# Gated linear attention and a soft mixture of experts: the turns go ahead of the scores in the middle units

## The chip, the cores and the metric

The kernel runs on one core of a Trainium2 chip. The metric is the device time of one execution in microseconds. The profile is one execution recorded by the hardware profiler; its times count from the start of its span.

## What is computed

Per batch (4) and head (8), over 768 positions of dimension 48, a gated linear attention; its output, as 3072 tokens of 384, goes through a soft mixture of 8 experts with 4 slots each.

```python
f = 1.0 / (1.0 + np.exp(-f_logit))
for t in range(S):
    state = f[:, :, t, :, None] * state + np.einsum('bhd,bhe->bhde', k[:, :, t], v[:, :, t])
    y[:, :, t] = np.einsum('bhd,bhde->bhe', q[:, :, t], state)
x = y.transpose(0, 2, 1, 3).reshape(B * S, H * D)
logits = x @ phi                                   # 3072 x 32
d = softmax(logits, axis=0); slot_input = d.T @ x  # 32 x 384
slot_out[e] = np.maximum(slot_input[e] @ w1[e], 0) @ w2[e]
out = softmax(logits, axis=1) @ slot_out
```

All data is fp32; w1 and w2 are 12.6 MB each.

## The kernel before

The positions are cut into chunks of 128; a unit is one chunk of 16 of the 32 head sequences, so there are 12 units (`NU`), and units u and u+2 share sequences. Two heads lie above each other on the 128 partitions, and 8 such pairs of 128 columns make the 1024 columns of a unit's f, k and q; half 0 is the first 512 columns, half 1 the rest.

The work on one unit, by the names in the code:

- The decay. `d_exp` and `d_ln` (ScalarE) make the log decay in the buffer of f; `d_scan` (VectorE) sums it up along the chunk; `d_g` makes its exponential g and `d_p` that of its negative, p (ScalarE). `d_k` multiplies k by g, `d_q` multiplies q by p (GpSimd; VectorE for unit 0). `d_pend` (ScalarE) keeps the last column of p for the state. In this kernel p has a region of its own and g is written over f.
- The scores. `scores(u, w)` are 8 matmuls over 48 rows for half w, into the PSUM tile PD (two banks). `s_mask` (VectorE) applies the causal mask on the way to SBUF. Both halves use PD, so the second scores wait for the first mask; only unit 0 puts its second half into the banks PA.
- The turns. `kt` turns k by 8 transposes into PC, `kt_copy` (ScalarE) takes it to SBUF for `kv`, which forms the chunk's addition to the state; `state_t` and `state_2` (VectorE) update the state. `x_tr` turns the outputs of the unit before into PA[0] and PA[1], and `x_copy` takes them out, the first half on ScalarE, the second on VectorE.
- The outputs. `inter` (queries by the old state) and `intra` (values by the masked scores) add up in PB, and `y_copy` (ScalarE) takes them to SBUF.
- Routing, once per two units. `c_lg` forms the logits in PA[0], `c_max` and `c_exp` a running softmax over the tokens, `c_tr` turns two 128x128 weight tiles in PB[0], `c_pin` sums the slots in PA[1], and `c_join` folds that into `pin`.

Every step has a due time, and `run_atoms` emits all steps in the order of their due times; `keep_order` fixes that order on each engine. So each engine works off its list strictly in order, and what stands at its head blocks what follows. The due times are written in the table `OFF`, in units whose period is T = 8.6; the frame of unit u begins at u*T with its first scores. Within frame u the decay of unit u+1 is finished (g, p, both products) and that of unit u+2 begun (exponential, logarithm, scan). Due times of units 0 to 4 are written out singly. In the old frame TensorE's order is: scores 0, turns of k, turns of x of the unit before, (odd frames: `c_tr`), scores 1, (even frames: `c_pin`, `c_lg`), `kv`, `intra` 0, `intra` 1; `inter` stands behind scores 1 in odd units and ahead of it in even ones.

SP issues nearly all transfers, in the same order of due times. f, k, q and v have 3, 3, 3 and 2 buffers; a load waits for the last reader of its buffer, and everything behind it on SP waits too. The w1 units (768 KB each) go into `wr` through the loop; w2 goes into the regions of f, p, k, q, v as these fall free, and six last ones into `wr` when `up` has read it.

After unit 11 the tail runs: `t_psi`, `up` (slots by w1), `turn`, then `down` in two column parts: part 0 (256 columns, PD) and part 1 (128 columns, PB[0]), 16 steps each. `slot_out` scales a part, `slot_out2` sums it over the experts and copies it to `s4`. `c_ct` turns the token softmax weights. `combine(h, y)` multiplies them by part h for a third y of the tokens, one bank for each of four row groups; ScalarE copies two banks, VectorE (`combine_2`) the other two, and `store` writes it out. Steps of the second `down` stand between the combines.

## Time and profile before

| | us |
|---|---|
| median of 3 runs | 155.72 (155.66 to 155.74) |
| the profiled execution | 155.44 |
| its span, first to last instruction | 153.7 |
| busy: TensorE matmul / weight load | 138.1 / 109.4 |
| busy: VectorE / ScalarE / GpSimd | 104.3 / 94.3 / 58.5 |
| moved by DMA | 53.97 MB |

The span is the time from the first to the last instruction on the core; 1.74 us of the profiled execution lie around it. In the rows, PE is TensorE's matmul and PEld its weight load, DVE is VectorE, ACT is ScalarE, POOL is GpSimd, and SPq is SP's DMA issue. An fp32 matmul leaves two records of each kind, a transpose one. "issue" behind a gap means that the engine waited for nothing that the profile shows. Most operands are called `arena`, which is one SBUF tile that holds all regions, so a step is told by its line: L185 `d_exp`, L188 `d_ln`, L193 `d_scan`, L196 `d_p`, L202 `d_g`, L206 `d_k`, L210 `d_q`, L219 `kt`, L222 `kt_copy`, L230 `scores`, L239 `s_mask`, L252 `kv`, L274 `inter`, L283 `intra`, L294 `y_copy`, L299 `x_tr`, L305 `x_copy`, L469 `down`, L482 `slot_out2`, L501 `combine`, L513 `store`.

### The profile page before, as it was taken

The numbers are of one execution on the slowest core, as the hardware profiler recorded it, in microseconds if no ns is written. First come the engines' busy times: TensorE is split into PE (matmuls) and PEld (weight loads), VectorE is DVE, ScalarE is ACT, GpSimd is POOL, SyncE is SP. The second block draws the span as 40 slices with busy tenths as digits, with TensorE's granted clock in tenths as the row PEclk, the third lists the DMA queues.
The fourth block names the chain that finished last, engine by engine and source line by source line (L and its number), as shares of the span: only waits on it lengthen the run. The fifth ranks groups of instructions, "written<-read, shape, count | busy, mean of one in ns | idle before, by whom it ended". The sixth has DMA issues, their size and how long they took to land.

```text
span 153.7 us, 5505 instructions
## 1 busy us (share of the span) xinstructions
PE 138.1 (90%) x2392; PEld 109.4 (71%) x2392; DVE 104.3 (68%) x153; ACT 94.3 (61%) x182; POOL 58.5 (38%) x51
## 2 busy tenths in 40 slices
PE   7987999999889999999999999999889999997500
PEld 7976888989769898889879897877433556675400
DVE  6899686999579887896969887759510563146500
ACT  4998899997789796969596976334402121035400
POOL 7008585788556483909293655600000000000000
PEclk9999999999999999999999999999999999999965
DMA  4899999999999999999999939999999993009990
GB/s 153 279 364 421 402 408 406 412 409 411 410 404 415 401 410 398 393 401 389 397 410 406 388 113 374 412 419 420 417 417 337 422 422 156 0 4 420 409 386 32
DMA packets 13424, 53.97 MB, mean 351 GB/s; under 512 B 1488, under 2 KB 1616, under 8 KB 13008
## 3 DMA queue, kind: packets, MB, share of 16 engines
q1 hardware_dynamic: 13248, 53.02, 87.2%
q10 hardware_dynamic: 144, 0.52, 0.9%
q8 instruction: 20, 0.33, 0.9%
q14 instruction: 12, 0.10, 0.2%
HBM read 48.82 MB, written 4.72 MB: 348 GB/s over the span
## 4 chain that ended last, share of the span: by engine, by line


## 5 line engine op out<-in xcount | busy, mean ns | idle before, releaser
L210 POOL TENSOR_TENSOR arena<-arena 128x512 f32<-128x512 f32 (+1 forms) x15 | 28.6, 1908 | 38.9 <-ACT arena L196 28.4
L239 DVE TENSOR_TENSOR arena<-pd,mask 128x1024 f32<-128x1024 f32 x23 | 27.8, 1210 | 10.2 <-PE pd L230 10.2
L193 DVE TENSOR_TENSOR_SCAN arena<-again,arena 128x512 f32<-128x512 f32 (+1 forms) x17 | 30.3, 1787 | 3.3 <-ACT arena L188 3.3
L230 PE MATMUL pd<-arena 48*128 48x128 f32 x368 | 27.0, 285 | 1.6 <-DVE arena L239 0.6
L206 POOL TENSOR_TENSOR arena<-arena 128x512 f32<-128x512 f32 (+1 forms) x15 | 27.6, 1852 | 0.4 <-POOL arena L206 0.4
L230 PEld LDWEIGHTS pd<-arena 48*128 48x128 f32 x368 | 22.3, 187 | 5.7 <-POOL arena L206 1.7
L283 PE MATMUL pb<-arena 128*48 128x128 f32 x384 | 23.5, 274 | 0.0
L283 PEld LDWEIGHTS pb<-arena 128*48 128x48 f32 x384 | 20.3, 123 | 1.1 <-issue 0.8
L196 ACT ACTIVATE arena<-arena 128x512 f32<-128x512 f32 (+1 forms) x17 | 13.6, 801 | 10.5 <-DVE arena L193 10.5
L294 ACT COPY arena<-pb 128x512 f32<-128x512 f32 x24 | 13.6, 584 | 6.6 <-PE pb L283 6.3
L185 ACT ACTIVATE arena<-arena 128x512 f32<-128x512 f32 (+1 forms) x16 | 13.5, 847 | 1.5 <-DMA arena<-in_f_dram 1.5
L202 ACT ACTIVATE arena<-arena 128x512 f32<-128x512 f32 (+1 forms) x17 | 13.8, 811 | 0.3
L188 ACT ACTIVATE arena<-arena 128x512 f32<-128x512 f32 (+1 forms) x16 | 13.5, 844 | 0.5
L299 PE MATMUL pa<-ident,arena 112*128 112x112 f32 x96 | 11.6, 262 | 0.3 <-ACT arena L294 0.3
L274 PE MATMUL pb<-arena 48*48 48x128 f32 x320 | 10.9, 274 | 0.0
L299 PEld LDWEIGHTS pa<-ident,arena 112*128 112x128 f32 x96 | 9.7, 141 | 1.1 <-ACT arena L294 0.7
L252 PE MATMUL pc<-arena 128*48 128x48 f32 x320 | 9.2, 210 | 0.9 <-ACT arena L222 0.9
L252 PEld LDWEIGHTS pc<-arena 128*48 128x48 f32 x320 | 8.1, 125 | 2.6 <-ACT arena L222 1.1
L219 PE MATMUL pc<-ident,arena 112*128 112x112 f32 x80 | 9.9, 266 | 0.0
L274 PEld LDWEIGHTS pb<-arena 48*48 48x48 f32 x320 | 8.4, 119 | 1.4 <-issue 0.2
L219 PEld LDWEIGHTS pc<-ident,arena 112*128 112x128 f32 x80 | 7.8, 141 | 1.9 <-issue 1.0
L165 PE MATMUL pd<-ones 128*128 128x128 f32 x50 | 7.3, 317 | 1.1 <-POOL ones L143 1.1
(140 smaller groups left out, 199.3 us busy)
## 6 DMA issues: line engine op xcount, KB each, us to landing
wr<-in_w_dram SPq DMA_DIRECT2D x22, 768.0 KB, 8.6
arena<-in_w_dram SPq DMA_DIRECT2D x10, 768.0 KB, 9.4
arena<-in_f_dram SPq DMA_DIRECT2D x10, 512.0 KB, 7.4
arena<-in_q_dram SPq DMA_DIRECT2D x10, 512.0 KB, 8.5
arena<-in_k_dram SPq DMA_DIRECT2D x10, 512.0 KB, 7.1
arena<-in_v_dram SPq DMA_DIRECT2D x12, 384.0 KB, 7.3
out_dram<-wr SPq DMA_DIRECT2D x3, 1024.0 KB, 4.8
arena<-in_f_dram SPq DMA_DIRECT2D x4, 256.0 KB, 4.1
```

The lines of the kernel that those rows point to most:

```text
L193: nc.vector.tensor_tensor_scan(t, cols(again, h), t, 0.0, op0=ALU.mult, op1=ALU.add)
L196: nc.scalar.activation(cols(R("p", u), h), cols(R("f", u), h), AF.Exp, scale=-1.0)
L202: nc.scalar.activation(cols(G(u), h), cols(R("f", u), h), AF.Exp)
L206: (eng or nc.gpsimd).tensor_tensor(t, t, cols(G(u), h), op=ALU.mult)
L210: (eng or nc.gpsimd).tensor_tensor(t, t, cols(R("p", u), h), op=ALU.mult)
L219: nc.tensor.transpose(PC[:, a // 4, 128 * (a % 4) : 128 * (a % 4) + W], kq[:W, a], ident[:W, :W])
L230: nc.tensor.matmul(t[:, 128 * p : 128 * p + 128], kq[rs, 4 * w + p], qq[rs, 4 * w + p], start=True, stop=True)
L239: nc.vector.tensor_tensor(dst, src, mask.unsqueeze(1).broadcast_to(list(dst.shape)), op=ALU.mult)
L252: nc.tensor.matmul(kvs[64 * r : 64 * r + D, a], kr[:, a, r], vb(u, a, r ^ a // 4), start=True, stop=True)
L274: nc.tensor.matmul(ys[a][o : o + D], heads(S0(u), D)[rs, a], qq[rs, a], start=p == 0, stop=False, skip_group_check=True,)
L283: nc.tensor.matmul(ys[4 * w + p][o : o + D], vb(u, 4 * w + p, r ^ w), sc[:, r, p], start=u < 2 and p == 0, stop=p == 3, skip_group_check=True,
L299: nc.tensor.transpose(PA[w][:, 128 * p : 128 * p + W], xTs[u][:W, w, p], ident[:W, :W])
```

## The change

1. Frames 4 to 9 (`BOTH`) take their due times from a second table, `OFF2`. TensorE's order there is: turns of k, turns of x, (`c_tr`), scores 0, scores 1, `inter`, (`c_lg`, `c_pin`), `kv`, `intra` 0, `intra` 1. The second scores of units 4 to 9 go into the banks PA[0] and PA[1], and their mask is two VectorE instructions of 512 columns instead of one of 1024.
2. p is written over f and g has the region of its own, everywhere; g and the product with k come before p and the product with q.
3. The second half of `x_copy` of units 3, 5 and 7 goes from VectorE to ScalarE (in the frames 4, 6 and 8).
4. Unit 5's logarithm stands behind the output copies of unit 3; its scan, both exponentials and products run by halves in frame 4. Unit 6's exponential and logarithm are placed by hand in that frame.
5. In the tail the turns of the second routing weights (`c_ct`) go from ahead of `down` step 8 to behind `slot_out(0)`; two steps of the second `down` stand ahead of the first combine instead of seven, then 5, 6 and 3 behind the combines instead of 3, 3 and 3; in `combine` the copy of the third bank is emitted after the first half of the matmuls.

```diff
+BOTH = range(4, 10)
+OFF2 = dict(
+    kt=0, xt=T + 0.82, tr=2 * T + 1.75, sc0=2.05, sc1=3.05, inter=4.15, lg=T + 5.2, pin=3 * T + 5.25, kv=5.4, intra0=5.7, intra1=6.6,
+    xe=T + 1.9, el=2 * T + 1.95, mask0=3.1, mask1=4.1, mx=T + 5.3, join=3 * T + 5.35, st=6.2, s2=6.3, scan=7.1 - 2 * T,
+    ktok=0.85, g=2.4 - T, p=3.5 - T, pend=4.6 - T, exp=4.7 - 2 * T, ln=5.8 - 2 * T, et=T + 6.0, y0=6.55, y1=7.55,
+    dk=3.0 - T, dq=4.4 - T,
+)
...
+    def d_g(u, h=None):
+        nc.scalar.activation(cols(R("g", u), h), cols(R("f", u), h), AF.Exp)
+
     def d_p(u, h=None):
-        nc.scalar.activation(cols(R("p", u), h), cols(R("f", u), h), AF.Exp, scale=-1.0)
...
+        nc.scalar.activation(cols(R("f", u), h), cols(R("f", u), h), AF.Exp, scale=-1.0)
...
-                rs, t = slice(64 * r, 64 * r + D), PD[:, r] if u or not w else PA[r]
+                rs, t = slice(64 * r, 64 * r + D), PA[r] if w and (not u or u in BOTH) else PD[:, r]
...
-        if u or not w:
+        if not w or u and u not in BOTH:
             parts = [(sc, PD.rearrange("p r (a t) -> p (r a) t", t=L))]
         else:
             parts = [(sc[:, 4 * r : 4 * r + 4], heads(PA[r], L)) for r in range(2)]
...
-            (nc.vector.tensor_copy if w and u < NU - 1 else nc.scalar.copy)(x, y)
+            (nc.vector.tensor_copy if w and u not in (3, 5, 7, NU - 1) else nc.scalar.copy)(x, y)
...
+            if n2 == 0:
+                combine_2(h, y, 2)
...
-        items += [(turn, 1, 0), (turn, 1, 1), (c_ct, 1)]
+        items += [(turn, 1, 0), (turn, 1, 1)]
         items += [(down, 0, *STEPS[x]) for x in range(8, 16)]
-        items += [(slot_out, 0)]
-        items += [(down, 1, *STEPS[x]) for x in range(3)]
-        items += [(slot_out2, 0)]
-        items += [(down, 1, *STEPS[x]) for x in range(3, 7)]
+        items += [(slot_out, 0), (c_ct, 1), (slot_out2, 0)]
+        items += [(down, 1, *STEPS[x]) for x in range(2)]
         for y in range(3):
...
-            items += [(down, 1, *STEPS[x]) for x in ((7, 8, 9), (10, 11, 12), (13, 14, 15))[y]]
+            items += [(down, 1, *STEPS[x]) for x in ((2, 3, 4, 5, 6), (7, 8, 9, 10, 11, 12), (13, 14, 15))[y]]
...
+        (2 * T + 2.955, d_exp, 5), (2 * T + 7.56, d_ln, 5), (3 * T + 2.0, d_scan, 5, 0), (3 * T + 2.1, d_g, 5, 0), (3 * T + 2.2, d_p, 5, 0),
+        (3 * T + 2.3, d_k, 5, 0), (3 * T + 2.4, d_q, 5, 0), (3 * T + 4.2, d_scan, 5, 1), (3 * T + 4.75, d_g, 5, 1), (3 * T + 4.76, d_p, 5, 1),
+        (3 * T + 4.77, d_k, 5, 1), (3 * T + 4.78, d_q, 5, 1), (3 * T + 4.8, d_pend, 5), (3 * T + 2.25, d_exp, 6), (3 * T + 4.7, d_ln, 6),
...
-    early = {(u, "inter"): u * T + 2.84 for u in (2, 4, 6, 8, 10, 11)}
+    early = {(u, "inter"): u * T + 2.84 for u in (2, 10, 11)}
```

(The times of the last list are counted from T, so 3 * T + 2.0 lies in frame 4.)

## Rows read from the trace of the kernel before

**Rows 1.** Stretches by frame; columns: engines' busy us (instructions), TensorE clock, DMA share, GB/s
```profile
38.91:49.26 10.35, 9.47 (x186) 7.81 (x184) 7.82 (x10) 8.60 (x18) 6.40 (x4) 1.00 1.03 410
...
49.26:56.98 7.72, 7.72 (x149) 6.94 (x147) 6.49 (x8) 6.39 (x11) 4.71 (x2) 1.00 1.03 409
...
56.98:66.12 9.14, 9.14 (x186) 7.81 (x184) 7.61 (x11) 7.23 (x14) 4.72 (x2) 1.00 1.01 396
...
82.98:90.70 7.72, 7.72 (x148) 6.93 (x146) 6.49 (x8) 6.34 (x10) 4.71 (x2) 1.00 0.83 323
```

**Rows 2.** Order of time, frame 5; columns: start, length, engine, line, operands, [idle before <-releaser]
```profile
49.26 0.97 PEld L230 LDWEIGHTS pd<-arena 48*128 48x128 f32 x16 [0.19 <-issue]
...
50.35 0.78 PEld L219 LDWEIGHTS pc<-ident,arena 112*128 112x128 f32 x8
```

**Rows 3.** Order of time: turns of k of unit 1, behind outputs
```profile
17.05 0.78 PEld L219 LDWEIGHTS pc<-ident,arena 112*128 112x128 f32 x8 [0.19 <-issue]
```

**Rows 4.** Order of time, frame 6: inter-chunk, then the second scores
```profile
59.75 0.84 PEld L274 LDWEIGHTS pb<-arena 48*48 48x48 f32 x32
...
60.77 0.97 PEld L230 LDWEIGHTS pd<-arena 48*128 48x128 f32 x16 [0.18 <-DVE arena L305]
```

**Rows 5.** Order of time, frame 4: logarithm, scan, second scores
```profile
39.13 1.06 ACT L188 ACTIVATE arena<-arena 128x1024 f32<-128x1024 f32 x1
...
40.29 2.45 DVE L193 TENSOR_TENSOR_SCAN arena<-again,arena 128x1024 f32<-128x1024 f32 x1 [1.54 <-ACT arena L188]
...
43.91 0.97 PEld L230 LDWEIGHTS pd<-arena 48*128 48x128 f32 x16 [0.73 <-DVE arena L239]
```

**Rows 6.** Order of time, ScalarE, frame 4: k copy, x copy, exponential
```profile
43.80 0.78 ACT L222 COPY arena<-pc 128x768 f32<-128x768 f32 x1
...
44.47 0.48 ACT L305 COPY arena<-pa 128x384 f32<-128x384 f32 x1
...
44.84 1.07 ACT L202 ACTIVATE arena<-arena 128x1024 f32<-128x1024 f32 x1
```

**Rows 7.** Order of time: scans on VectorE and products on GpSimd
```profile
34.86 1.72 DVE L193 TENSOR_TENSOR_SCAN arena<-again,arena 128x512 f32<-128x512 f32 x1
...
35.45 2.20 POOL L206 TENSOR_TENSOR arena<-arena 128x512 f32<-128x512 f32 x1
...
48.70 2.28 DVE L193 TENSOR_TENSOR_SCAN arena<-again,arena 128x1024 f32<-128x1024 f32 x1
...
54.55 2.37 POOL L206 TENSOR_TENSOR arena<-arena 128x1024 f32<-128x1024 f32 x1
...
56.49 2.58 DVE L193 TENSOR_TENSOR_SCAN arena<-again,arena 128x1024 f32<-128x1024 f32 x1
```

**Rows 8.** Order of time: second scores of unit 10
```profile
93.97 0.97 PEld L230 LDWEIGHTS pd<-arena 48*128 48x128 f32 x16 [0.42 <-DVE arena L239]
```

**Rows 9.** Groups by line and shape: count, busy us, mean ns, idle before
```profile
L305 DVE COPY arena<-pa 128x384 f32<-128x384 f32 x11 | 6.0, 548 | 0.5 <-PE pa L299 0.3
...
L239 DVE TENSOR_TENSOR arena<-pa,mask 128x512 f32<-128x512 f32 x2 | 1.3, 680 | 0.0
```

**Rows 10.** Order of time: last down steps, first combine, first store
```profile
134.00 0.81 PEld L469 LDWEIGHTS pb<-arena 128*32 128x32 f32 x32 [0.33 <-issue]
...
134.10 0.37 ACT L482 COPY s<-pd 128x256 f32<-128x256 f32 x1 [4.51 <-PE pd L481]
...
135.01 0.18 PEld L501 LDWEIGHTS pc<-s,ct 32*128 32x128 f32 x1 [0.20 <-issue]
...
136.89 0.18 PEld L501 LDWEIGHTS pd<-s,ct 32*128 32x128 f32 x1 [0.20 <-issue]
...
136.94 0.18 PEld L501 LDWEIGHTS pa<-s,ct 32*128 32x128 f32 x1
...
137.54 0.35 SPq L513 DMA_DIRECT2D out_dram<-wr  x1
```

**Rows 11.** Stretches: the output transfers at the end, columns as in the first group
```profile
138.50:149.50 11.00, 4.80 (x106) 3.43 (x94) 4.67 (x11) 3.59 (x6) 0.00 (x0) 0.91 1.00 404
```

More of the change, by code (lines that the diff above doesn't have):

```diff
@@ L47 @@
     lf=-1.7 - 3 * T, lk=4.0 - 3 * T, lq=6.4 - 3 * T, lv=-T,
-    exp=4.45 - 2 * T, ln=5.6 - 2 * T, scan=7.1 - 2 * T, p=1.0 - T, dq=2.05 - T, g=3.3 - T, dk=4.4 - T, pend=4.35 - T,
+    exp=4.45 - 2 * T, ln=5.6 - 2 * T, scan=7.1 - 2 * T, g=1.0 - T, dk=2.05 - T, p=3.3 - T, dq=4.4 - T, pend=4.35 - T,
     sc0=0, mask0=1.05, kt=1.1, ktok=1.95, sc1=2.85, mask1=3.95, inter=4.9, kv=5.4, intra0=5.7, st=6.2, s2=6.3, y0=6.55, intra1=6.6, y1=7.55,
@@ L97, in gla_soft_moe_kernel @@
     region("f", NF, 1024)
-    region("p", NP_, 1024)
+    region("g", NP_, 1024)
     region("kt", 1, 768)
@@ L490, in gla_soft_moe_kernel, with combine @@
     ]
-    def combine(h, y, last=(2, 3)):
+    def combine(h, y, last=True):
         hs_, wc = slice(CO[h], CO[h] + WC[h]), WC[h]
@@ L496, in combine @@
         banks = [two[:, 0], two[:, 1], b2, b3]
+        dst = stage[h][:, 2 * y : 2 * y + 2]
         for n2 in range(2):
@@ L501, in combine @@
                     nc.tensor.matmul(banks[n][:, wc * x : wc * x + wc], ct[ns, 2 * y + x], s4[ns, hs_], start=True, stop=True)
-        dst = stage[h][:, 2 * y : 2 * y + 2]
+            if n2 == 0:
+                combine_2(h, y, 2)
         nc.scalar.copy(dst[:, :, :2].rearrange("p v n d -> p n v d"), two[:, :, : 2 * wc].rearrange("p n (v d) -> p n v d", v=2))
-        for n in last:
-            combine_2(h, y, n)
+        if last:
+            combine_2(h, y, 3)
     def combine_2(h, y, n):
@@ L585, in gla_soft_moe_kernel @@
         (d_k, 0, 0, V), (d_q, 0, 0, V), (scores, 0, 0), (d_k, 0, 1, V), (d_q, 0, 1, V), (scores, 0, 1),
-        (load, "f", f, 3), (d_exp, 1, 0), (d_ln, 1, 0), (d_exp, 1, 1), (d_ln, 1, 1), (d_pend, 0), (kt, 0), (d_scan, 1, 0), (d_p, 1, 0), (d_scan, 1, 1), (kt_copy, 0),
-        (s_mask, 0, 0), (d_q, 1, 0), (d_g, 1, 0), (d_k, 1, 0), (d_p, 1, 1), (d_g, 1, 1), (d_k, 1, 1), (d_q, 1, 1), (s_mask, 0, 1), (kv, 0), (intra, 0, 0),
+        (d_exp, 1, 0), (d_ln, 1, 0), (d_pend, 0), (load, "f", f, 3), (d_exp, 1, 1), (d_ln, 1, 1), (kt, 0), (d_scan, 1, 0), (d_g, 1, 0), (d_scan, 1, 1), (kt_copy, 0),
+        (s_mask, 0, 0), (d_k, 1, 0), (d_p, 1, 0), (d_q, 1, 0), (d_g, 1, 1), (d_p, 1, 1), (d_k, 1, 1), (d_q, 1, 1), (s_mask, 0, 1), (kv, 0), (intra, 0, 0),
         (scores, 1, 0), (y_copy, 0, (0,)), (state_2, 0), (d_exp, 2, 0), (d_ln, 2, 0), (intra, 0, 1), (s_mask, 1, 0), (y_copy, 0, (1,)), (kt, 1),
-        (d_scan, 2, 0), (d_exp, 2, 1), (d_ln, 2, 1), (x_tr, 0), (d_pend, 1), (d_p, 2, 0), (d_q, 2, 0), (scores, 1, 1), (d_scan, 2, 1), (kt_copy, 1),
-        (d_g, 2, 0), (d_k, 2, 0), (s_mask, 1, 1), (d_p, 2, 1), (d_g, 2, 1), (d_k, 2, 1), (x_copy, 0), (intra, 1, 0), (kv, 1), (intra, 1, 1), (d_q, 2, 1),
+        (d_scan, 2, 0), (d_exp, 2, 1), (d_ln, 2, 1), (x_tr, 0), (d_pend, 1), (d_g, 2, 0), (d_k, 2, 0), (scores, 1, 1), (d_scan, 2, 1), (kt_copy, 1),
+        (d_p, 2, 0), (d_q, 2, 0), (s_mask, 1, 1), (d_g, 2, 1), (d_p, 2, 1), (d_k, 2, 1), (x_copy, 0), (intra, 1, 0), (kv, 1), (intra, 1, 1), (d_q, 2, 1),
         (state_2, 1), (d_pend, 2), (y_copy, 1), (d_exp, 3), (d_ln, 3),
@@ L615, in gla_soft_moe_kernel @@
         ):
-            if u < 2 or u == 2 and key in done or u in (3, 4) and key in ("exp", "ln", "scan", "p", "g", "dq", "dk") or u > NU - 3 and key in last_state:
+            if u < 2 or u == 2 and key in done or u in (3, 4, 5) and key in ("exp", "ln", "scan", "p", "g", "dq", "dk") or (u, key) in ((5, "pend"), (6, "exp"), (6, "ln")) or u > NU - 3 and key in last_state:
                 continue
-            at(early.get((u, key), z + o[key]), fn, u, *args)
+            frame = u - (2 if key in ("exp", "ln", "scan") else 1 if key in done else 0)
+            at(early.get((u, key), z + off(frame, key)), fn, u, *args)
         if 0 < u < NU - 1:
-            at(z + o["xt"], x_tr, u)
-            at(z + o["xe"], x_copy, u)
+            at(z + off(u + 1, "xt"), x_tr, u)
+            at(z + off(u + 1, "xe"), x_copy, u)
     for g in range(NV - 1):
@@ L625, in gla_soft_moe_kernel @@
         for key, fn in (("lg", c_lg), ("mx", c_max), ("et", c_exp), ("tr", c_tr), ("el", c_copy), ("pin", c_pin), ("join", c_join)):
-            at(z + o[key] - (T if g == NV - 2 and key in ("pin", "join") else 0), fn, g)
+            frame = 2 * g + (2 if key in ("lg", "mx", "et") else 3)
+            at(z + off(frame + (key in ("pin", "join")), key) - (T if g == NV - 2 and key in ("pin", "join") else 0), fn, g)
     at(-3, load_phi)
@@ L641, in gla_soft_moe_kernel @@
         [9 * T + 6.9, 10 * T + 6.9, 10 * T + 4.5, 10 * T + 4.6, 10 * T + 4.0, 11 * T + 4.0, 10 * T + 6.4, 11 * T + 6.4, 12 * T - 0.5],
-        span("f", 2) + span("p", 2) + span("k", 2) + span("q", 2) + span("v"),
+        span("f", 2) + span("g", 2) + span("k", 2) + span("q", 2) + span("v"),
     ))
```

22 lines of the change are left out of this document (10 added, 12 removed).

## The prediction

> **What bounds the kernel now.** I read the stretches by frame first: a frame runs from one unit's first scores to the next unit's. Frames 4, 5 and 6 last 10.35, 7.72 and 9.14 us, and the pair 7.72 and 9.14 repeats to frame 9; from 5 on TensorE is busy in all of it while VectorE, ScalarE and GpSimd are not (6.5, 6.4 and 4.7 of 7.72) [rows 1]. So TensorE's stream sets the loop: an odd frame has one piece more (two turns of the routing weights), an even one two (slot sums and logits). The transfers look full (share 1.01 to 1.03) but are not what waits: in frame 9 they run dry, at share 0.83 and 323 GB/s, and TensorE still takes its 7.72 us [rows 1].
>
> The time inside TensorE's stream that can be won is small. Weight loads are busy 6.94 of 7.72 us [rows 1]; the rest are gaps of 0.12 to 0.20 us where one piece ends and one of another operand shape begins. Scores to turns of k: 49.26 + 0.97 to 50.35, 0.12 us [rows 2]. Outputs to turns of k: 0.19 us at 17.05 [rows 3]. Inter-chunk to scores: 0.18 us [rows 4]. They stand there too where nothing was waited for ("issue"), so the change of shape makes them and not the wait.
>
> Frame 4 is another matter. ScalarE's logarithm of unit 5 ends at 40.19, the whole scan runs 40.29 to 42.74 behind it, the first mask comes after that on VectorE, and the second scores, which share the mask's PSUM tile, start at 43.91 after 0.73 us of idle loads [rows 5].
>
> From 138.5 on the output transfers are the bound (share 1.00, 404 GB/s for 11 us) [rows 11], so the end moves with the first store, at 137.54 [rows 10], as long as the next ones come in time.
>
> **Steady frames 5 to 9, part by part.** New TensorE order: turns of k, turns of the last unit's x, (routing turns), scores, scores, inter-chunk, (logits, slot sums), state, outputs. The gap between scores and the turns of k (0.12) goes. The gap before the turns does not: they now follow the outputs, and that costs the same 0.19 [rows 3] as outputs to scores did [rows 2]. The gap inter-chunk to scores (0.18) comes back as inter-chunk to logits. Scores to scores has one shape, bounded by 0 and 0.18; I take 0, since inside a run of one shape the 16 loads stand without a hole [rows 2]. So 0.12 us a frame: 7.60 and 9.02.
>
> Who could take this back? (a) The second scores now write the two banks that the x turns use, so they wait for both x copies. In even frames both are ScalarE's: the k copy can start at 1.02 into the frame (turns 0.98 long), the first x copy follows 0.67 later, the second 0.37 after it (44.47 behind 43.80 shows the first step, the next ScalarE instruction at 44.84 the second), end 0.48 on: 2.54 [rows 6]. TensorE gets there at 1.68 + 0.97 = 2.65, where 1.68 is both turns (59.75 - 56.98 - 1.09) [rows 1, 4]. Cover 0.1 us: thin, but enough. In odd frames VectorE copies one half behind its scan, ending near 2.0 + 0.55 = 2.55, against 2.9. (b) The second mask becomes two instructions of 0.68 [rows 9] for one of about 1.2 (42.74 to 43.91 in [rows 5]), so some 0.15 us more on VectorE, which idles 1.2 us a frame [rows 1]; taking a 0.55 us x copy [rows 9] off it in frames 4, 6 and 8 more than pays. Logits must wait for the first of them: 2.85 + 1.2 + 0.68 = 4.73, just when TensorE arrives. (c) GpSimd now does k before q. k is wanted at the frame's start, q 1.7 us later, so both products have cover; before, the second ended at 54.55 + 2.37 = 56.92, 0.06 us ahead of the scores it feeds at 56.98 [rows 1, 7]. (d) p now lives in the buffer of f, so the load of f three units on waits for the q product, up to 0.9 us into the next frame. SP holds the next v and w1 behind it. f is read in the second frame after, so this is free. Exchanging the exponentials of units 0 to 3 swaps equal instructions, and the scores still wait for the same second product: 0.
>
> **Frame 4.** Unit 5's exponential goes ahead into a ScalarE wait, its logarithm behind the y copies, its scan is cut in halves. TensorE: both turns to 38.91 + 1.68 = 40.59, first scores to 41.56. ScalarE: the last y copy of unit 3 follows the outputs that end about 38.95 (0.6 us, an estimate from 0.48 for the x copy's 384 columns [rows 6]) and ends about 39.6, logarithm 1.06 [rows 5] to 40.65, k copy, x copies at 41.3 and 41.65, to 42.15 [rows 6]. So the second scores start at about 42.2 instead of 43.91, still 0.6 late. Then scores and gap 1.09, inter-chunk 1.02 [rows 4], and what followed the second scores before, 49.26 - 43.91 - 1.09 = 4.26: 48.57. Frame 4 goes from 10.35 to 9.65: **-0.70**. Its bounds: 0 if the half scans and the final chain mask, join, state end late, -0.9 if the x copies were ready.
>
> **Frame 5** inherits a late VectorE. Unit 6's scan starts at about 48.2, at the same moment as GpSimd's last half product of unit 5. What two such cost each other: a half scan took 1.72 us over a half product of 2.20 [rows 7], where halves of 2.37 and 2.28 are 1.2 and 1.15; a whole scan with 0.43 us of overlap took 2.58 instead of 2.28 [rows 7]. So I add 0.65, nearer the half scan's, since the overlap is near 1.2 us: scan to 51.15, x copy to 51.7, while TensorE wants the bank at 48.57 + 2.9: 0.3 of stall. Frame 5: 7.72 - 0.12 + 0.3, **+0.17**.
> [...]
>
> **Frames 6 to 9**: 4 x 0.12 = **-0.48**. **Frame 10** returns to the old order with scores first, so unit 10 needs q at once. Scan to 2.0 into frame 9, exponential 1.06, two products of 2.37 [rows 5, 7]: about 7.95, where TensorE is ready at 7.60: **+0.35**. In exchange the second scores of unit 10, which stood 0.42 for the mask [rows 8] where a bare gap is 0.18, no longer do: **-0.24**. Loop: -0.70 + 0.17 - 0.48 + 0.35 - 0.24 = -0.90.
>
> **The end.** Seven steps of the second down projection stood before the first combine, now two; and the turns of the routing weights go from the wait for the j=1 mask to the wait for the scaled slots, so they fill another hole and cost nothing. The four steps behind the slot sum took 134.00 to 135.01, 0.20 each with a gap of 0.20 [rows 10]. With two the combine is bound by ScalarE's copy (134.10 + 0.37 = 134.47) [rows 10] and starts at 134.6 instead of 135.01: **-0.40**. Copying the third bank after half the matmuls gains nothing: the weights of the first bank (pd) and of the last (pa) go in within 0.05 us, at 136.89 and 136.94 [rows 10], so the four banks fill side by side. So the first store goes 0.4 earlier. The later combines move up to 0.55 back, because more steps now stand between them, but each 1 MB store hides 2.6 us of that. Bounds 0 to -0.6.
>
> **Sum.** -0.90 - 0.40 = -1.30. The profiled execution took 155.44 (span 153.7, 1.74 around it), the median is 155.72, so 154.14 and **154.4**.
>
> **Rivals.** (1) Slower: VectorE becomes the bound. Its busy time per pair of frames is 6.49 + 7.61 = 14.10 [rows 1]; with the masks' +0.30 and the x copy's -0.55 it is 13.85. If both whole scans of a pair ran wholly over GpSimd products, stretched like the half scan (1.72 for 1.2), they add some 1.6: 15.4; with 2.0 of its 2.76 idle us kept, since masks and state must wait for TensorE, a pair takes 17.4 against 16.86. Two and a half pairs: +1.4, frame 4 and the end give back 1.1, the wait at frame 10 is in it: **156.1**. It decides from the point where the scans end later than 2.6 into the frame. For it: the q product now reaches 0.3 to 0.9 us into the next frame. Against it: its overlap is 0.85 us and only every second frame. (2) No change: frame 4's stall only moves (late half scans, late join and state) and stores 2 and 3 starve the output queue. Gains 0.48 less 0.3: **155.5**. (3) More: score to score and outputs to turns both cost no gap, 0.19 in six frames: **153.3**.
>
> **How the numbers follow.** Forecast 0.55, (1) 0.18, (2) 0.15, (3) 0.12. Its own range is 153.7 to 155.2. With the rivals 153.2 to 156.2, which leaves out some 0.17. A measurement of this kernel tells 0.2% (0.3 us) from no change. Faster: forecast, (3) and a little of (2), 0.68; same 0.13; slower 0.19.
>
> **What would show it.** Right: odd frames near 7.6 and even ones near 9.0, each beginning with turns behind a 0.19 gap, no gap between the two scores; second scores of unit 4 near 42.2, waiting for ScalarE; scores of unit 10 waiting for GpSimd; first store 0.4 earlier relative to the last down step. Wrong: second scores waiting for x copies in most frames, scans of 2.8 us or more, a hole in the output transfers, or a frame 4 still over 10 us.

## The result and the profile after

The changed kernel takes **156.76 us** (median of 20 runs) against 155.95 for the kernel before, measured beside it: a ratio of 1.0056, 95% interval 1.0034 to 1.0078. It is slower by about 0.8 us where 1.3 us of gain was forecast. The profiled execution took 157.69 (span 155.9, 1.8 around it); it is one of the longer of its 20 runs, so it shows rather more loss than the median has.

In the rows of the changed kernel and of the runs made from it the lines are L201 `d_scan`, L215 `d_q`, L224 `kt`, L235 `scores`, L244 `s_mask`, L257 `kv`, L288 `intra`, L304 `x_tr`, L365 `c_pin`, L435 the copies behind `turn`, L468 `c_ct` and L474 `down`.

First the stretches by frame, as in [rows 1] (columns: engines' busy us, TensorE clock, DMA share, GB/s). Frame 4 is 39.61 to 50.71, the last row is frame 10.

```profile
39.61:50.71 11.10, 9.73 (x186) 8.17 (x184) 7.99 (x11) 9.06 (x18) 6.27 (x5) 1.00 1.02 410
50.71:58.23 7.52, 7.52 (x149) 6.86 (x147) 6.65 (x9) 6.67 (x10) 4.28 (x2) 1.00 1.01 395
58.23:67.26 9.03, 9.03 (x186) 7.75 (x185) 7.89 (x11) 7.96 (x15) 5.14 (x3) 1.00 0.99 380
67.26:75.39 8.13, 7.82 (x148) 6.91 (x146) 7.25 (x9) 6.68 (x10) 4.70 (x2) 1.00 0.99 377
75.39:84.42 9.03, 9.03 (x185) 7.75 (x184) 7.27 (x11) 7.86 (x15) 4.71 (x2) 1.00 1.02 400
84.42:92.42 8.00, 7.59 (x149) 6.86 (x147) 7.12 (x9) 7.03 (x11) 4.70 (x2) 1.00 0.77 311
92.42:100.50 8.08, 7.80 (x144) 6.33 (x144) 7.21 (x10) 3.61 (x9) 4.71 (x2) 1.00 0.87 322
```

The steady frames came as forecast: 7.52 for 7.72 and 9.03 for 9.14. Two frames did not: frame 4 grew from 10.35 to 11.10 instead of shrinking to 9.65, and frame 7 has 8.13. Frame by frame against before: +0.70 up to frame 4, then +0.75, -0.20, -0.11, +0.41, -0.11, +0.28, 0.00; from frame 11 to the last step of the first `down` part 0.00; from there to the end +0.44 (21.76 for 21.32). The +0.70 ahead of frame 4 is not the change: over all profiles here frame 4 begins between 38.91 and 39.74 with the old loop (six runs, mean 39.31) and between 38.86 and 39.80 with the new one (nine runs with the old warm-up, mean 39.31); in nine of these fifteen VectorE waits 0.2 to 1.0 us for the second half of unit 0's k.

The loss in frame 4 stands in TensorE's order of time, in the middle of the state matmuls `kv` (columns: start, length, engine, line, operands, [idle before <-releaser]):

```profile
45.78 0.83 PE L365 MATMUL pa<-arena,el 128*32 128x384 f32 x8
46.54 0.74 PE L257 MATMUL pc<-arena 128*48 128x48 f32 x23
48.61 0.42 PE L257 MATMUL pc<-arena 128*48 128x48 f32 x9 [1.33 <-issue]
```

TensorE stops after 23 of the step's 32 matmul records and goes on 1.54 us later (start to start), in a run of equal matmuls whose operands are all there. "issue" means that the profile shows nothing that was waited for. Frame 7 has a smaller one inside `intra`:

```profile
73.91 0.35 PEld L288 LDWEIGHTS pb<-arena 128*48 128x48 f32 x5
74.82 0.39 PEld L288 LDWEIGHTS pb<-arena 128*48 128x48 f32 x7 [0.56 <-issue]
```

Counted from the start of TensorE's records (matmuls, weight loads and its few waits, 4817 in all), both holes begin at a record that is 193 over a multiple of 256 (1473 and 2497), and so does the hole of 0.40 that the kernel before has inside its 16 scores at 40.47 (record 1217). The DMA queues have a row for code: 20 transfers, 0.33 MB, so 16 KB each; 20 blocks of 256 would hold the 4817 records. From 13 to 111 us exactly one of these transfers begins between each such block's end and the next.

```profile
q8 instruction: 20, 0.33, 0.9%
```

So I formed the **theory** that TensorE runs out of code: a block of 256 instructions is fetched by DMA, and where it comes late the engine stands at the block's end. In the trace the block that TensorE goes on with at 48.61 began to be fetched at 46.06, which is 4.96 us after the last block's end at 41.11; the transfer takes about 1.1 and another 1.5 pass until the engine goes on. Without holes a block lasts 5.8 to 7.3 us in the loop, 6.0 in frame 4, so by my estimate (6.0 less 1.1 and 1.5) a delay above about 3.5 is felt there. The **rivals**: the hole belongs to that place in the work; or the loss is the tail's.

### The profile page after: what moved, and what is told of

Its sections match the earlier page's. It is cut to its first block, busy times and chain, and to the rows that moved or that the text cites. A ratio compares the mean times of both kernels' runs of the same rounds, so it can differ in the third digit from the quotient of the medians.

```text
span 155.9 us, 5541 instructions
## 1 busy us (share of the span) xinstructions
PE 138.2 (89%) x2392; PEld 109.5 (70%) x2392; DVE 106.0 (68%) x157; ACT 98.0 (63%) x187; POOL 58.4 (37%) x53
## 3 DMA queue, kind: packets, MB, share of 16 engines
q1 hardware_dynamic: 13248, 53.02, 86.5%
## 4 chain that ended last, share of the span: by engine, by line
## 5 line engine op out<-in xcount | busy, mean ns | idle before, releaser
L201 DVE TENSOR_TENSOR_SCAN arena<-again,arena 128x512 f32<-128x512 f32 (+1 forms) x18 | 32.7, 1820 | 3.9 <-ACT arena L196 3.9
L215 POOL TENSOR_TENSOR arena<-arena 128x512 f32<-128x512 f32 (+1 forms) x16 | 28.9, 1804 | 0.0
L244 DVE TENSOR_TENSOR arena<-pd,mask 128x1024 f32<-128x1024 f32 x17 | 20.6, 1214 | 8.0 <-PE pd L235 8.0
L288 PE MATMUL pb<-arena 128*48 128x128 f32 x384 | 23.9, 274 | 0.3 <-issue 0.3
L288 PEld LDWEIGHTS pb<-arena 128*48 128x48 f32 x384 | 20.4, 123 | 1.6 <-issue 1.4
L235 PE MATMUL pd<-arena 48*128 48x128 f32 x272 | 19.8, 285 | 1.3 <-POOL arena L215 0.4
L235 PEld LDWEIGHTS pd<-arena 48*128 48x128 f32 x272 | 16.5, 187 | 4.5 <-POOL arena L215 1.8
L257 PEld LDWEIGHTS pc<-arena 128*48 128x48 f32 x320 | 8.2, 125 | 5.4 <-issue 4.3
L304 PE MATMUL pa<-ident,arena 112*128 112x112 f32 x96 | 11.7, 262 | 0.3 <-ACT arena L299 0.3
L257 PE MATMUL pc<-arena 128*48 128x48 f32 x320 | 9.4, 210 | 2.2 <-issue 1.3
L304 PEld LDWEIGHTS pa<-ident,arena 112*128 112x128 f32 x96 | 9.7, 141 | 1.1 <-ACT arena L299 0.7
L224 PE MATMUL pc<-ident,arena 112*128 112x112 f32 x80 | 9.9, 266 | 0.0
L227 ACT COPY arena<-pc 128x768 f32<-128x768 f32 x10 | 7.9, 792 | 1.9 <-PE pc L224 1.9
L244 DVE TENSOR_TENSOR arena<-pa,mask 128x512 f32<-128x512 f32 x14 | 9.0, 681 | 0.1
```

What stands on the lines that cost most here:

```text
L201: nc.vector.tensor_tensor_scan(t, cols(again, h), t, 0.0, op0=ALU.mult, op1=ALU.add)
L215: (eng or nc.gpsimd).tensor_tensor(t, t, cols(R("f", u), h), op=ALU.mult)
L235: nc.tensor.matmul(t[:, 128 * p : 128 * p + 128], kq[rs, 4 * w + p], qq[rs, 4 * w + p], start=True, stop=True)
L244: nc.vector.tensor_tensor(dst, src, mask.unsqueeze(1).broadcast_to(list(dst.shape)), op=ALU.mult)
L257: nc.tensor.matmul(kvs[64 * r : 64 * r + D, a], kr[:, a, r], vb(u, a, r ^ a // 4), start=True, stop=True)
L288: nc.tensor.matmul(ys[4 * w + p][o : o + D], vb(u, 4 * w + p, r ^ w), sc[:, r, p], start=u < 2 and p == 0, stop=p == 3, skip_group_check=True,
```

## The experiments

**Which half loses.** Two runs take the change apart: the new loop with the old end, and the old loop with the new end. (Edit: `tail` and `combine` of the one kernel put into the other.)

> The changed loop with the old end (old order of the down steps, weight turns and bank copies). The profile of the changed kernel had its first store 0.44 us earlier against the last step of the first down part, as predicted, but its last store 0.64 later and the end of the span 0.48 later (21.82 against 21.34). Theory (the new end costs about 0.4, because the last store sets the end): 156.3 against the changed kernel's 156.76. Rival (the new end gains the predicted 0.4 and the loop loses all): 157.2. Third (the end is worth nothing either way, stragglers of the last transfers): 156.8. The span from the last step of the first down part to the end tells the same in the profile: 21.3 (theory) or 21.8.

> The kernel before with the new end alone. Theory (new end costs 0.4): 156.4 against 155.95. Rival (gains the predicted 0.4): 155.55. Third: 155.95.

Measured: the new loop with the old end 1.0049 (1.0019 to 1.0079), the old loop with the new end 0.9978 (0.9956 to 1.0000). The loop is what loses; the end gains 0 to 0.7. That the end costs 0.4 fell; what it does is settled further down. The new loop has its hole again, at the same place in the state matmuls: 1.54 us, with the code fetched 5.07 after the block's end.

**Is the hole code?** One run leaves out four loads, so that less stands in the queues around frame 4; two others shift the block ends by 64 records.

```diff
     def load_w1(i):
         e, hf = W1[i]
         w1u[e, hf] = wr[:, i].rearrange("p (c x) -> p c x", c=3)
+        if i in (2, 3, 4, 5):
+            w1u[e, hf] = wr[:, 0].rearrange("p (c x) -> p c x", c=3)
+            return
```

> The changed kernel without the loads of four of the sixteen w1 units (the third to the sixth, 768 KB each, whose matmuls read the first unit instead), which leaves out 7.9 us of transfers in frames 3 to 5. Theory (code for TensorE comes late because its transfer stands behind data in busy queues): the code blocks start within 2 us of the last block's end in frames 3 to 5, there is no hole in unit 4's state matmuls, and frame 4 is at most 9.7 us instead of 11.10. Rival (code comes late for a reason of its own, or the hole isn't code): hole and frame stay, 11.1. The whole time falls by an amount that tells nothing, since transfers are left out.

Measured: the hole is gone. The stretches of frames 4 and 5, the step where the hole was, and the queues from the block's end at 40.76 (columns: transfers, which the profile's page calls packets, MB, share):

```profile
39.27:48.80 9.53, 9.49 (x186) 8.05 (x184) 7.58 (x11) 8.36 (x17) 5.04 (x5) 1.00 0.85 287
48.80:56.73 7.93, 7.78 (x148) 6.93 (x146) 6.97 (x9) 7.20 (x12) 7.78 (x3) 1.00 0.45 164
```

```profile
46.20 0.93 PE L257 MATMUL pc<-arena 128*48 128x48 f32 x32
```

```profile
q1 hardware_dynamic: 14, 0.04, 72.6%
q8 instruction: 1, 0.02, 41.4%
```

The code block was fetched 0.10 us after the last one ended, behind 14 data transfers, fewer than one for each of the 16 DMA engines; in the changed kernel 4.96 us, behind 517 (32 for each). Frames 4 to 10 sum to 59.12 against 59.87 before. So without late code the new loop is worth **0.75 us**; in the changed kernel they sum to 60.89. (The paced run further down keeps all transfers and has the same 59.12.)

The two shifts:

```diff
-        warm(25, PD[:, 1, :128])
+        warm(41, PD[:, 1, :64])
```

> The changed kernel with 41 warm-up matmuls of 64 columns ahead of the first scores instead of 25 of 128, so that every later TensorE instruction stands 64 records further on in the instruction stream (4 records each) and the work is the same. Theory (the holes of 1.46 us in the state matmuls of unit 4 and 0.56 in the outputs of unit 7 are TensorE running out of code: each hole stands where a fetched block of 256 instructions ends): those two places run through without a hole, and any hole of this kind stands 64 records earlier in the work (with a block's end at about 46.9 instead of 48.6 in frame 4, that is in the slot sums or before them). Rival (the holes belong to the work there, a wait that the profile doesn't show): they stay at the same matmuls. Time: theory, 156 to 157, by where the ends now fall; rival 156.8.

```diff
+    def pad(n):
+        for _ in range(n):
+            nc.tensor.matmul(PC[:, 1, 496:512], ones, ones[:, :16], start=True, stop=True)
...
-        (d_k, 0, 0, V), (d_q, 0, 0, V), (scores, 0, 0), (d_k, 0, 1, V), (d_q, 0, 1, V), (scores, 0, 1),
+        (d_k, 0, 0, V), (d_q, 0, 0, V), (scores, 0, 0), (pad, 8), (d_k, 0, 1, V), (d_q, 0, 1, V), (scores, 0, 1),
...                                         # and (pad, 8) behind (kt, 0)
```

> The changed kernel with 16 matmuls of 16 columns (64 records) added in two holes of TensorE ahead of 14 us, so that the ends of the code blocks stand 64 records earlier in the work, with the clock as it was. Theory (blocks of 256): no hole in the middle of unit 4's state matmuls nor in the outputs of unit 7; a hole, if the backlog still makes one, stands 64 records earlier, in unit 4's slot sums at about 46.5, or at the ends of the other blocks. Rival (the hole belongs to that place in the work): unit 4's state matmuls stop after 23 or 24 of 32 as before. Time by the theory 155.5 to 157, by the rival 156.8.

Measured: 169.11 and 163.84 us, so both times were missed by far, because TensorE was slow until 24 and 28 us (last section). In both, `kv` of unit 4 and `intra` of unit 7 run through, and no block end in frames 4 to 10 has a hole above 0.10. That speaks against a hole that belongs to its place. At the start of frame 4 as much had been moved as in the changed kernel (14.32 and 14.36 MB, 14.32 there), but the code came 3.31 and 3.19 us after the block's end instead of 4.96, so no hole shows at the shifted place either, and these two alone would not decide.

**With all transfers kept.** The w1 loads are spread otherwise, in the new loop and, as a control, in the old.

```diff
     for i in range(16):
-        at((1.6 + 0.62 * i) * T - 0.9, load_w1, i)
+        at((1.6 + 0.62 * (i + 2 * (3 <= i < 12))) * T - 0.9 if i not in (12, 13) else 9 * T + 6.8, load_w1, i)
```

> The changed kernel with the same transfers, but the w1 units from the fourth on are issued two places (10.7 us) later and the thirteenth and fourteenth go into the hole that the transfers have in frame 9 (10 GB/s from 91.5 to 94). Theory (the loop's loss is TensorE waiting for blocks of its code, which stand behind the backlog of data): without the loads of the four w1 units the same loop took 9.53, 7.93, 9.03, 7.52, 9.03, 8.00 and 8.08 us for frames 4 to 10, 59.12 against 59.87 before, so with a shorter backlog in frames 3 to 5 frame 4 is at most 9.7, the hole in unit 4's state matmuls goes, and the median is 155.95 - 0.75 - 0.1 (the end): 155.1. Rival (the holes only move to another frame as the loads come later): 156.7. Second rival (the loss in the median sits elsewhere, the hole is an accident of the profiled execution): 156.7 with all frames short.

> The kernel before with the same later w1 loads. Theory (in the kernel before the one late block of code, at 40.47, lies under the wait for the first mask, so there is nothing to win): 155.95, within 0.3. Rival (the later loads are worth something of themselves, so that a gain of the run before this is not the changed loop's): 155.2 or less.

Measured: 0.9995 (0.9970 to 1.0020) in the new loop, where the changed kernel has 1.0056, and 1.0005 (0.9979 to 1.0032) in the old. So the spread takes 0.6% off the new loop and nothing off the old: the hole was the loss. Frame 4 of the paced run, with the code now 3.61 after the block's end:

```profile
38.88:48.42 9.54, 9.50 (x186) 8.06 (x185) 7.59 (x11) 8.36 (x17) 5.09 (x5) 1.00 0.98 361
```

But 155.1 was missed by 1 us. The 0.76 that frames 4 to 10 give are there at the first `down` step (123.33 for 124.09), and 0.23 of them are left at the last step of its first part (132.15 for 132.38): TensorE, now early, stands for the last w2 units.

```profile
130.61 1.43 PEld L474 LDWEIGHTS pd<-wr,arena 128*32 128x32 f32 x26 [0.40 <-DMA wr<-in_w_dram]
```

The kernel before has no such wait. The transfers run full from 54 to 128 us here; the new pacing has a hole of its own at 50 to 54 (16 GB/s from 50 to 52). Two variants of the paced run: frame 9 in the old order (`BOTH = range(4, 9)`), and the old end.

> The later w1 loads of the first of these runs, and frame 9 in the old order (frames 4 to 8 alone begin with the turns). Theory (frame 9 costs 0.28 because unit 10, which begins with scores, finds its q product 0.41 late): frame 9 back to 7.72 and no wait for GpSimd ahead of unit 10's scores, 0.28 below the first run: 154.8. Rival (frame 9 in the old order gives back its turn gap of 0.12 and the stretched scan of unit 11 comes earlier anyway): equal to the first run within 0.1.

> The paced run of the changed loop (w1 two places later) with the old end. Theory (in the new end the turns of the weights cost 0.44 because they lost their cover, and with the old end they stand in the wait for the mask and for the last w2 units): 0.4 below the paced run with the new end (156.07), 155.65, and 21.3 instead of 21.76 from the last step of the first part. Rival (the end is the same either way, its transfers set it): 156.05.

Measured: 0.9991 (0.9965 to 1.0017) and 1.0007 (0.9982 to 1.0033), both equal to the paced run, so both theories missed their times. In the first, frame 9 is 7.71 instead of 7.99 and nothing stands before unit 10's scores, as expected; holes of 0.17 and 0.15 for code and the wait for w2 take it back. In the second the code block of frame 4 came 4.05 late and made a hole of 0.44, so it does not tell the ends apart.

**The end.** Old place for the weight turns, five steps instead of seven ahead of the first combine, in the old loop and in the new:

```diff
-        items += [(down, 1, *STEPS[x]) for x in range(3, 7)]
+        items += [(down, 1, *STEPS[x]) for x in range(3, 5)]
...
-            items += [(down, 1, *STEPS[x]) for x in ((7, 8, 9), (10, 11, 12), (13, 14, 15))[y]]
+            items += [(down, 1, *STEPS[x]) for x in ((5, 6, 7, 8, 9), (10, 11, 12), (13, 14, 15))[y]]
```

> The kernel before; of the second down part five steps instead of seven stand ahead of the first combine, the weight turns stay in their old place ahead of the last steps of the first part, and the two steps go between the first and the second combine. The first combine and the first store come 0.4 earlier (2.2 instead of 2.63 after the last step of the first part), the later combines and the last store stay (9.67; last store 12.74). Theory (the end follows the last store: in all profiles so far it comes 8.4 to 8.8 us after that store is issued): end 21.3 after the last step of the first part as before, time 156.0. Rival (the prediction's: the transfers are full, so the end moves with the first store): 20.9, time 155.6.

> The changed kernel with the end in which the weight turns stay in their old place and five steps stand ahead of the first combine. Theory (the new end gave back its 0.4 because the weight turns lost the wait that covered them; with it the output stream from first to last packet takes 13.66 us instead of 13.28): first combine still 2.2 after the last step of the first part, stream 13.28, last output packet 0.4 earlier than in the changed kernel, 156.3 against 156.76. Rival (the closing code after the last packet takes that up): 156.7.

Measured: 0.9993 (0.9963 to 1.0023) in the old loop, 1.0023 (0.9994 to 1.0053) in the new, which lies 0.3% under the changed kernel, with intervals that overlap. The traces say more. In five runs with the old end the output stream takes 13.27 to 13.30 us from its first to its last packet and ends 19.27 to 19.30 after the last step of the first part; in five with the new end (all but the shift runs and the one without four loads) 13.65 to 13.68 and 19.19 to 19.23; with this one 13.28 and 18.85 (old loop), 13.12 and 18.68 (new loop). So for the stream the prediction's rule (the first store moves it) held, the theory that the last store sets it fell, and the new end's stream has a hole. In the time it is not shown: the stream's 0.44 would be 0.9972 in the old loop, and the interval holds that as well as no change. First the old loop's stretch of full output with this end, then that of the changed kernel and the hole in it:

```profile
138.80:150.10 11.30, 5.39 (x118) 3.95 (x114) 5.10 (x11) 3.95 (x6) 0.00 (x0) 0.94 1.01 409
```

```profile
139.70:151.20 11.50, 5.96 (x142) 4.59 (x138) 5.10 (x11) 3.95 (x6) 0.00 (x0) 1.00 0.98 394
143.90:145.10 1.20, 0.84 (x24) 0.69 (x26) 0.21 (x1) 0.27 (x1) 0.00 (x0) 1.00 0.79 328
```

From the last packet to the end another 2.0 to 2.7 us pass, in which blocks of code are fetched again; they vary by more than what is to be told apart here, which is why single spans do not settle the end.

**All three causes together.** The changed loop without frame 9, this end, and w1 loads that leave no hole in the transfers; and, as a control, the same loads and end with the old loop.

```diff
-        at((1.6 + 0.62 * i) * T - 0.9, load_w1, i)
+        at(4 * T + 6.5 if i in (4, 5) else 9 * T + 6.8 if i > 12 else (1.6 + 0.62 * (i + (2 if i == 3 else i > 5))) * T - 0.9, load_w1, i)
```

> The changed loop with frame 9 in the old order, the end of the run before this, and w1 loads spread anew: the fourth a frame later, the fifth and sixth at the end of frame 4 where the paced runs had a hole in the transfers (16 GB/s from 50 to 52), the last three into the hole of frame 9. Theory (three things took the loop's 0.75 in turn: late code, then the last w2 units, which TensorE reached 0.35 ahead of their landing, then the turns of the weights out of their cover, 0.44): no hole for code, no wait for w2, end 21.3 after the first part's last step: 156.0 - 0.75 - 0.28 = 155.0, ratio 0.993 to 0.995. Rival (the transfers from 2 to 129 us are a bound of their own, so that TensorE's gains before them are lost in the wait for w2 whatever the order): 155.7 or more, with a wait for w2 of 0.3 or more.

> The fastest run's spread of the w1 loads and its end, with the loop of the kernel before. Theory (the changed loop is worth 0.75 to 1.0 once code and w2 come in time): 155.8 to 156.0, against 155.02 with the changed loop. Rival (the gain of that run is the spread of the loads and the end, the loop's order is worth nothing in the time): 155.0 to 155.3.

Measured: **155.02 us, 0.9924 (0.9898 to 0.9950)** with the changed loop, the fastest here, and 0.9979 (0.9952 to 1.0005) with the old one. So the loop, without frame 9, is worth about 0.55% (0.85 us; 0.2 to 0.9% by the two intervals together) once its code and w2 come in time. Its frames 4 and 5, and the sum of frames 4 to 10:

```profile
39.02:48.75 9.73, 9.69 (x186) 8.17 (x185) 7.78 (x11) 8.56 (x18) 5.27 (x5) 1.00 0.98 353
48.75:56.49 7.74, 7.74 (x148) 6.93 (x147) 6.74 (x9) 7.00 (x11) 7.47 (x3) 1.00 1.03 385
...
sum 58.83, PE 58.64 PEld 50.82 DVE 50.44 ACT 48.50 POOL 36.54; mean PE 8.38 PEld 7.26 DVE 7.21 ACT 6.93 POOL 5.22
```

58.83 against 59.87 before, and no wait for w2 behind it. That is the forecast's 0.75 + 0.28, although a hole of 0.17 for code is left. Its end missed the forecast: 21.94 for 21.3, since the output stream has a straggler (99% of the bytes are out 17.28 after the last step of the first part, for 17.97 before, but the last packet at 19.45). So the gain shown is the loop's and not the end's.

**What makes the code late.** Two runs tried to turn the delay up and down: w1 loads one place earlier in the kernel before, and two single w1 loads of the changed kernel moved away from a block's end.

```diff
-        at((1.6 + 0.62 * i) * T - 0.9, load_w1, i)                        # kernel before
+        at((1.6 + 0.62 * (i - (i > 1))) * T - 0.9, load_w1, i)
...
-        at((1.6 + 0.62 * i) * T - 0.9, load_w1, i)                        # changed kernel
+        at({4: 4 * T + 5.2, 9: 7 * T + 6.1}.get(i, (1.6 + 0.62 * i) * T - 0.9), load_w1, i)
```

> The kernel before with the w1 units from the third on issued one place (5.3 us) earlier, so that about 2 us more of data stand in the queues in every frame from 3 on. Theory (code for TensorE stands behind the backlog of data): the blocks of code that were fetched 3.1 to 3.7 us after the last block's end in frames 3 to 6 come some 1 to 2 us later still, and the kernel before gets holes of 0.5 us and more of the kind 'issue' in frames 4 to 7 that it did not have: 156.5 to 158. Rival (the fetch time has nothing to do with the backlog): no new hole, 156.0.

> The changed kernel with two of the sixteen w1 loads issued some 3.5 to 4 us later and nothing else moved: the fifth (issued at 41.25, just as a code block ended at 41.1) and the tenth (issued at 67.76, as one ended at 68.3). Theory (the code waits for data that SP has just put into the queues): the fetches come 3.0 to 3.7 us after the block's end instead of 4.96 and 4.22, frame 4 is at most 9.7 instead of 11.10 and frame 7 at most 7.6 instead of 8.13, and the time is 0.7 to 1.2 below the changed kernel: 155.6 to 156.1. Rival (the fetch waits for whatever is in flight, of which there is as much as before): fetches as late, frame 4 above 10.5, 156.7.

Measured: 0.9989 (0.9956 to 1.0022), no new hole; and 1.0038 (1.0012 to 1.0064), the hole of frame 4 unchanged. Both expectations of the theory fell. More data in the queues (3.48 MB issued and not yet moved at the block's end in frame 4, against 3.13 in the kernel before) left the delay at 3.74 (3.67), and in frame 4 the moved load left it at 4.99. The changed kernel itself had less in its queues at that point than the kernel before, 1.86 MB, and its code came later all the same. Frame 7's hole went (fetch 2.10 late), but in two runs where nothing was moved there it is also gone or down to 0.14 (fetch 2.93 and 3.56 late). What the traces do show is how many data transfers pass ahead of the code. The kernel before, the one with earlier loads, and the changed one, each from the block's end in frame 4 to the fetch:

```profile
q1 hardware_dynamic: 396, 1.52, 101.7%
q8 instruction: 1, 0.02, 1.9%
```

```profile
q1 hardware_dynamic: 377, 1.55, 101.4%
q8 instruction: 1, 0.02, 1.9%
```

```profile
q1 hardware_dynamic: 517, 2.06, 102.9%
q8 instruction: 1, 0.02, 1.3%
```

That is 25, 24 and 32 for each of the 16 DMA engines. It is no fixed number: at the next four block ends of the kernel before it is 20, 14, 14 and 20, with the DMA engines as full, and while they are full the count says the same as the delay. The hole follows the delay from run to run:

| run | code fetched after the block's end in frame 4 | hole |
|---|---|---|
| changed kernel; with the old end; two w1 moved; new end mended | 4.96; 5.07; 4.99; 4.97 | 1.54 each |
| paced, old end | 4.05 | 0.44 |
| fastest; paced without frame 9 | 3.77; 3.68 | 0.17 each |
| paced | 3.61 | 0.04 |
| four w1 loads left out | 0.10 | none (0.04) |

Why 32 transfers go first in the one and 24 in the others stays open. The paced runs differ from the others in the fourth w1 load, which the latter issue at 34.9 to 35.5, well ahead of the block's end; that load alone was not tried.

## Why the prediction was wrong, point by point

Two steps failed. The prediction's reading that the transfers "are not what waits" put TensorE's waits for its code at nothing, and in frame 4 they cost 1.54 us, 1.1 net. And the moved weight turns, which were to "cost nothing", came to stand in TensorE's time, and the second down part ends 0.65 later after the last step of the first.

- **What bounds the loop.** "TensorE's stream sets the loop" was right, but not all of the stream's time is its work. That the transfers "are not what waits" was looked at for data alone; TensorE's code comes over the same DMA engines (row q8: 0.9% of the time of the same 16). The sign stood in the trace of before, where TensorE stops inside its 16 equal scores:

```profile
38.91 1.16 PE L230 MATMUL pd<-arena 48*128 48x128 f32 x15
40.47 0.27 PE L230 MATMUL pd<-arena 48*128 48x128 f32 x1 [0.40 <-issue]
```

I had put "issue" down to a change of shape, which inside one shape it can't be. There it was hidden, since the mask waited for the scan until 42.74 [rows 5]; in the changed kernel the late block ends in `kv`, where nothing hides it.
- **Steady frames**, -0.12 each: right about the gaps. 7.52 (7.60 forecast) and 9.03 (9.02). The second scores start 0.88 behind the first (52.62 to 53.50) and not 0.97, which is the rest of the odd frames' gain; in the even ones the pieces behind them take 0.09 more than the sum had, so 9.02 was met with some luck. The gap ahead of the turns stayed, 0.19 as in [rows 3], and score to score has none:

```profile
50.71 0.78 PEld L224 LDWEIGHTS pc<-ident,arena 112*128 112x128 f32 x8 [0.19 <-issue]
51.44 0.81 PEld L304 LDWEIGHTS pa<-ident,arena 112*128 112x128 f32 x8
...
52.62 0.97 PEld L235 LDWEIGHTS pd<-arena 48*128 48x128 f32 x16 [0.17 <-issue]
53.50 0.98 PEld L235 LDWEIGHTS pa<-arena 48*128 48x128 f32 x16
```


The x copies were in time in these frames, so (a) and (b) held, and so did the 0 for the exchanged exponentials.
- **Frame 4**, -0.70: the step itself was right and even too cautious, 9.53 where the code comes in time for 9.65. The second scores start 2.85 us into the frame (3.29 forecast). What was missing is a term: +1.54 for the hole, of which frame 5 gives 0.42 back by then finding everything ready (7.52 for 7.94).
- **Frame 5**, +0.17: 7.94 in the paced run, +0.22; the size was right and the mechanism was not. The stall of 0.34 is not the scan's that runs late over a product, but the product's that runs late behind the scan:

```profile
51.64 0.97 PEld L235 LDWEIGHTS pa<-arena 48*128 48x128 f32 x16 [0.34 <-POOL arena L215]
```

```profile
48.17 2.34 DVE L201 TENSOR_TENSOR_SCAN arena<-again,arena 128x1024 f32<-128x1024 f32 x1
```

```profile
48.32 3.27 POOL L215 TENSOR_TENSOR arena<-arena 128x512 f32<-128x512 f32 x1
```


The scan starts 0.15 ahead, keeps its 2.34, and the product, 1.27 alone, ends 1.08 after it. So it stood for the scan rather than ran beside it.
- **Frame 9**, +0.35 for unit 10's wait: right, +0.28 with a wait for GpSimd. (The terms given, 2.0 + 1.06 + 2 x 2.37, make 7.80 and not the 7.95 that the forecast used; measured 8.00.) **Frame 10**, -0.24: wrong, 0.00. The second scores' wait of 0.42 for the mask [rows 8] came again. I had let the scores move back and the mask stand still; but the mask follows a scan that moved back too, and that lay over a later q product:

```profile
92.42 0.97 PEld L235 LDWEIGHTS pd<-arena 48*128 48x128 f32 x16 [0.66 <-POOL arena L215]
...
95.68 0.97 PEld L235 LDWEIGHTS pd<-arena 48*128 48x128 f32 x16 [0.42 <-DVE arena L244]
```

```profile
91.38 3.13 DVE L201 TENSOR_TENSOR_SCAN arena<-again,arena 128x1024 f32<-128x1024 f32 x1
94.44 1.19 DVE L244 TENSOR_TENSOR arena<-pd,mask 128x1024 f32<-128x1024 f32 x1
```

- **The end**, -0.40: the first combine came 0.44 earlier after the last step (2.19 for 2.63), the first store too, and the early copy of the third bank gained nothing, all as forecast. The step that failed is "they fill another hole and cost nothing". In the kernel before the turns (L463) stood ahead of the steps that wait for the j=1 mask. In the changed one that hole is still there, empty, and the turns stand behind the last step, in TensorE's time. First before, then after:

```profile
128.59 0.49 PE L463 MATMUL pa<-ident,el 128*128 128x128 f32 x3
129.10 0.41 PE L469 MATMUL pd<-arena 128*32 128x256 f32 x2
```

```profile
130.82 0.41 PE L474 MATMUL pd<-arena 128*32 128x256 f32 x2 [0.34 <-DVE arena L435]
```

```profile
134.41 0.55 PE L468 MATMUL pa<-ident,el 128*128 128x128 f32 x3
```


So from the last step to the last step of the second part 8.73 us pass instead of 8.08, the combines of part 1 come 0.65 later, the stores run dry at 144, and 0.06 of the 0.40 is left in the output stream. That each store hides 2.6 us of the later combines' delay was worked out for one store at a time, and it did not hold for the third. With the turns in their old place the whole 0.44 came in the stream and the 8.08 was back. (That end also has five steps instead of two ahead of the first combine and the old order of the bank copies, so no run changes the turns' place alone; their row is 0.55 long.)
- **Rivals.** The slower end came true, but not by VectorE: no scan held TensorE in frames 6 to 8. "No change" was near in its second half (stores starve the queue). None had the code, so the range to 156.2 rested on causes that did not come.
- **The sum.** Loop -0.75 for -0.90 without the hole; the hole +1.1 net in frame 4, and in the profiled execution 0.6 in frame 7; the end -0.06 in the stream for -0.40. Without frame 7's hole, which other runs of this loop lack, that makes +0.3 for the +0.8 of the median; the rest stays open.

## What to carry to other kernels

A gap marked "issue" inside a run of equal instructions is no change of shape: look whether such gaps stand at equal distances in the instruction stream (here a multiple of 256 records), and whether code is among the transfers; here, under full DMA queues, late code was a bound that lay under another wait (0.40 us in the kernel before) until the change removed that wait (1.54 us). A step that is moved out of a hole leaves the hole behind, so its cost in the new place is its whole length unless a hole of that length is shown there (here a row of 0.55, and 0.65 more up to the last step of the second part). And a gain on TensorE ahead of a stage that waits for transfers has to be followed to that stage: here 0.53 of 0.76 us stood again before the last weights until the loads were spread anew.

## What the runs showed of the hardware that was not expected

**Code shares the DMA engines with data.** The page of the changed kernel counts both against the same 16 engines: data 86.5% (q1), code 0.9% (q8) of their time. With the DMA engines full a block of 16 KB is fetched 0.88 (frame 5) to 4.96 us (frame 4 of the changed kernel) after the last one ends; with four loads left out, at a share of 0.73, once after 0.10. The amount queued does not set it (0.35 MB more, 0.07 us later; 1.27 MB less, 1.29 us later); 5 to 32 data transfers for each DMA engine go first. What makes it so many is not shown: no run here tells in what order one DMA engine takes data and code or how transfers are bundled (the profile calls each of them a packet), and the counts are averages over 16 engines.

**A scan and a product that overlap ran one after the other.** In [rows 7] I read 1.72 and 2.20 as two operations that slow each other down. In order of time the half product ahead of them on GpSimd ends at 35.48:

```profile
34.21 1.27 POOL L210 TENSOR_TENSOR arena<-arena 128x512 f32<-128x512 f32 x1 [0.47 <-DMA arena<-in_k_dram]
35.45 2.20 POOL L206 TENSOR_TENSOR arena<-arena 128x512 f32<-128x512 f32 x1
```

35.48 and a half scan of 1.1 to 1.2 (1.22 beside no product, at 41.38 in the changed kernel) make 36.6, the end of the scan that began at 34.86; the second product ends at 37.65, 1.07 behind that, where it takes 1.27 alone. The rows of frame 5 above show the same, with the scan first and the product's end 1.08 behind it; so some 0.2 of a product is not held up. So in both the later one stood for the earlier, and the prediction's reading of the rows, in which both are slowed, was not right; the 0.65 that it added to the scan of frame 5 did not come, because there the scan began first (2.34) and the product took 3.27.

**TensorE's clock in the shift runs.** In the second one, behind eight matmuls of 16 columns that follow the first scores, the granted clock is at half until about 28 us (0.50 of full from 14 to 28):

```profile
8.50:11.00 2.50, 2.50 (x30) 2.26 (x29) 2.13 (x4) 2.31 (x8) 0.00 (x0) 1.00 1.03 367
11.00:28.00 17.00, 16.11 (x135) 14.77 (x135) 6.85 (x8) 6.72 (x14) 5.00 (x4) 0.52 0.67 262
28.00:34.00 6.00, 6.00 (x106) 5.49 (x104) 3.47 (x4) 5.38 (x12) 4.78 (x4) 0.94 0.66 227
```

The granted clock falls at 11.67 us and is back at 28.73. In the first one, with the warm-up of 64 columns, the first scores took 438 ns each instead of 285, as long as those of the second run at half clock (438), and the slow stretch lasts to about 24 us. The trace has no record of the granted clock before 23.79 us there, where it begins at full (1.00); the column shows 1.00 where it has no record. In the changed kernel the record begins at 4.37 us, and the 25 warm-up matmuls of 128 columns are over by 8.8.
